# A decode block's result kept as columns, four neighbouring outputs per partition, and stored from there in 8-byte pieces

## The chip, the cores and the metric

One core of a Trainium2 (trn2) chip. The metric is device time in microseconds (us) of one execution. Runs of one kernel mostly agree within 0.3%, with single runs up to 0.5% above that. The profile shows one execution; its span is some 1.8 us shorter than the time of the same run, because the time also counts what lies around the span.

## The reference, cut to what matters

```python
def reference(A_x, A_k_cache, A_v_cache, A_wq, A_wo, B_x, B_w_gate, B_w_up, B_w_down):
    x = A_x                                              # [1, 1, 1024] bf16
    h = x + A_ref(layernorm(x), k_cache, v_cache, wq, wo)  # 32 query heads, 4 kv heads, 65,536 keys of 128
    return h + (gelu(hn @ w_gate) * (hn @ w_up)) @ w_down  # hn = layernorm(h), 3,584 hidden
```

It is one token through one block. Nearly all the work is reading 173 MB: the key and value caches, then the weights. The result is a single vector of 1,024 bf16 values, 2 KB. This document is about how that vector gets formed and stored.

Of the kernel before, what the change touches and what calls it, by code (L numbers as in the profile page):

```python
# [9 lines left out]
ALU = mybir.AluOpType  # L10
AX = mybir.AxisListType
BF16 = mybir.dt.bfloat16
# [5 lines left out]
def kernel(  # L18
# [13 lines left out]
    nc = tc.nc  # L32
    P = 128
    D = A_x.shape[-1]
# [5 lines left out]
    DC = D // P  # L40
# [19 lines left out]
    lead = ctx.enter_context(tc.tile_pool(name="lead", bufs=1))  # L60
    ones_f = lead.tile([P, P], F32, name="ones_f")
    ident_f = lead.tile([P, P], F32, name="ident_f")
    esel = lead.tile([P, 2, P], BF16, name="esel")
    qsel = lead.tile([P, Hkv, 2, 2, 32], BF16, name="qsel")
    hsel = lead.tile([P, 2], F32, name="hsel")
    sel = lead.tile([P, 32], F32, name="sel")
    x_pc = lead.tile([P, DC], F32, name="x_pc")
    x_cp = lead.tile([P, DC], F32, name="x_cp")
    x_row = lead.tile([DC, P], BF16, name="x_row")
    ident_bf = lead.tile([P, P], BF16, name="ident_bf")  # L70
    x_pc_bf = lead.tile([P, DC], BF16, name="x_pc_bf")
    xn_bf = lead.tile([P, DC], BF16, name="xn_bf")
    neg_half = lead.tile([P, 1], F32, name="neg_half")
# [1 line left out]
    xnz = lead.tile([P, DC, 32], BF16, name="xnz")  # L75
    chpool = ctx.enter_context(tc.tile_pool(name="chpool", bufs=NBUF))
    const = ctx.enter_context(tc.tile_pool(name="const", bufs=1))
    small = ctx.enter_context(tc.tile_pool(name="small", bufs=2))
    ps_m = ctx.enter_context(tc.tile_pool(name="ps_m", bufs=1, space=PSUM))
    actx = ExitStack()  # L80
# [9 lines left out]
    def load(src, name):  # L90
        t = chpool.tile([P, CW], BF16, name=name, tag="ch")
        n, w = src.shape[1], src.shape[2]
        tv = t[:, 0:n * w].rearrange("p (n w) -> p n w", w=w)
        nc.sync.dma_start(out=tv, in_=src)
        return tv
# [2 lines left out]
    WB = max(1, CW // HD)  # L98
    assert HD <= CW and DC % WB == 0
    nc.scalar.dma_start(out=x_pc_bf[:], in_=A_x[0, 0].rearrange("(p c) -> p c", c=DC))  # L100
    nc.scalar.dma_start(out=x_row[:], in_=A_x[0, 0].rearrange("(c p) -> c p", p=P))
    wq_tiles = []
    for c0 in range(0, DC, WB):
        wv = load(wq_v[:, c0:c0 + WB, :], "wq_sb")
# [23 lines left out]
    def layernorm_cols(src_col, dst_bf, tagp):  # L128
        s1 = small.tile([P, 1], F32, name=f"{tagp}_s1", tag="ln_s1")
        nc.vector.tensor_reduce(out=s1[:], in_=src_col, axis=AX.X, op=ALU.add)  # L130
        tot = ps_m.tile([P, 1], F32, name=f"{tagp}_tot", tag="misc")
        nc.tensor.matmul(tot[:], lhsT=ones_f[:], rhs=s1[:], start=True, stop=True)
        mean = small.tile([P, 1], F32, name=f"{tagp}_mean", tag="ln_mean")
        nc.vector.tensor_scalar(out=mean[:], in0=tot[:], scalar1=1.0 / D, scalar2=None, op0=ALU.mult)
        xc = small.tile([P, DC], F32, name=f"{tagp}_xc", tag="ln_xc")
        nc.vector.tensor_scalar(out=xc[:], in0=src_col, scalar1=mean[:, 0:1], scalar2=None, op0=ALU.subtract)
        sq = small.tile([P, DC], F32, name=f"{tagp}_sq", tag="ln_sq")
        s2 = small.tile([P, 1], F32, name=f"{tagp}_s2", tag="ln_s2")
        nc.vector.tensor_tensor(out=sq[:], in0=xc[:], in1=xc[:], op=ALU.mult)
        nc.vector.tensor_reduce(out=s2[:], in_=sq[:], axis=AX.X, op=ALU.add)  # L140
        tot2 = ps_m.tile([P, 1], F32, name=f"{tagp}_tot2", tag="misc")
        nc.tensor.matmul(tot2[:], lhsT=ones_f[:], rhs=s2[:], start=True, stop=True)
        ve = small.tile([P, 1], F32, name=f"{tagp}_ve", tag="ln_ve")
        nc.vector.tensor_scalar(out=ve[:], in0=tot2[:], scalar1=1.0 / D, scalar2=eps, op0=ALU.mult, op1=ALU.add)
        rstd = small.tile([P, 1], F32, name=f"{tagp}_rstd", tag="ln_rstd")
        nc.gpsimd.tensor_tensor(out=rstd[:], in0=ve[:], in1=neg_half[:], op=ALU.pow)
        nc.vector.tensor_scalar(out=dst_bf, in0=xc[:], scalar1=rstd[:, 0:1], scalar2=None, op0=ALU.mult)

    nc.vector.tensor_copy(out=x_pc[:], in_=x_pc_bf[:])
    layernorm_cols(x_pc[:], xn_bf[:], "ln1")  # L150
    xT_ps = ps_m.tile([P, DC], BF16, name="xT_ps", tag="misc")
    nc.tensor.transpose(out=xT_ps[:], in_=x_row[:], identity=ident_bf[0:DC, 0:DC])
    nc.vector.tensor_copy(out=x_cp[:], in_=xT_ps[:])

    def padded(pool, vec, ncols, name, t=None):
        if t is None:
# [35 lines left out]
    for hf in range(2):  # L192
        for t in range(2):
            o = W2 * hf + rep * t
            nc.vector.tensor_copy(out=qsel[64 * t:64 * t + 64, :, :, hf, o:o + rep],
                                  in_=qsel_ps[64 * t:64 * t + 64, :, :].rearrange("p a (g h) -> p g a h", h=rep))
# [148 lines left out]
    for dq in range(OQ):  # L345
        nc.tensor.matmul(o2_ps[:], lhsT=osel[:, dq, :], rhs=o_sb[:, dq * Hq:(dq + 1) * Hq],
                         start=(dq == 0), stop=(dq == OQ - 1))

    actx.close()
    rows = ctx.enter_context(tc.tile_pool(name="rows", bufs=1))  # L350
# [7 lines left out]
    def pair_mm(bank, stat, w2, c, first, last):  # L358
        for s in range(DS):
            g = 2 * s + c % 2  # L360
            nc.tensor.matmul(bank[32 * g:32 * g + 32, :], lhsT=stat, rhs=w2[:, s * 512:(s + 1) * 512],  # L361
                             start=first, stop=last, tile_position=(0, 32 * g))
# [6 lines left out]
    for wc in range(Hq // WN):  # L369
        wv = load(wo_v[:, wc * WN:(wc + 1) * WN, :], "wo_sb")  # L370
        for cc in range(WN):
            c = wc * WN + cc
# [4 lines left out]
    for s in range(DS):  # L377
        for c in range(DC):
            nc.tensor.matmul(hc_ps[64 * s:64 * s + 64, c:c + 1], lhsT=at_r[:, c::DC], rhs=hsel[:, s:s + 1],
                             start=True, stop=True, tile_position=(0, 64 * s))  # L380
# [6 lines left out]
    def cp_sum(row, add, name):  # L387
        ps = ps_t.tile([P, 4, DS], F32, name=name + "_ps", tag="T")
        for b in range(4):
            nc.tensor.matmul(ps[:, b, :], lhsT=row[:, b * P:(b + 1) * P], rhs=hsel[:], start=True, stop=True)  # L390
        t = rows.tile([P, DC], F32, name=name)
        nc.vector.tensor_tensor(out=t[:].rearrange("p (s b) -> p b s", b=4), in0=ps[:],
                                in1=add[:].rearrange("p (s b) -> p b s", b=4), op=ALU.add)
        return t

    h_cp = cp_sum(at_r, x_cp, "h_cp")

    assert F <= CW and FC == 28
# [43 lines left out]
    act_bf = rows.tile([P, FC], BF16, name="act_bf")  # L442
# [8 lines left out]
    d_ps = row_bank("d_ps")  # L451
    dl_ps = ps_w.tile([P, DC], F32, name="dl_ps", tag="w")
    nc.vector.memset(dl_ps[:], 0.0)
    o_blk = rows.tile([P, 32], BF16, name="o_blk")
    nc.vector.memset(o_blk[:], 0.0)
    o_tr = rows.tile([32, P], BF16, name="o_tr")
    c0 = 0
    for sz in sizes:
        wv = load(wd_v[:, c0:c0 + sz, :], "wd_sb")
        for cc in range(sz):  # L460
            c = c0 + cc
            if c < NW:
                pair_mm(d_ps, actz[:, c, :], wv[:, cc, :], c, c < 2, c + 2 >= NW)
                continue
            for j in range(DC):
                nc.tensor.matmul(dl_ps[:, j:j + 1], lhsT=wv[:, cc, j * P:(j + 1) * P], rhs=act_bf[:, c:c + 1],
                                 start=False, stop=False, skip_group_check=True)
        c0 += sz
        if c0 == NW:
            d_r = rows.tile([P, 512], F32, name="d_r")  # L470
            nc.vector.tensor_copy(out=d_r[:], in_=d_ps[:])
            hd_cp = cp_sum(d_r, h_cp, "hd_cp")
    nc.vector.tensor_tensor(out=o_blk[:, 0:DC], in0=dl_ps[:], in1=hd_cp[:], op=ALU.add)
    for i in range(4):
        nc.vector.transpose(out=o_tr[:, 32 * i:32 * i + 32], in_=o_blk[32 * i:32 * i + 32, :])
    nc.sync.dma_start(out=out[0, 0].rearrange("(c p) -> c p", p=P), in_=o_tr[0:DC, :])


# [28 lines left out]
```

## The kernel before: the parts that the change touches

The last matrix, `w_down`, comes in five loads of 14, 7, 4, 2 and 1 row groups. The first 14 groups are multiplied with the weights as the moving operand (`d_ps`). The sums of this bank, four partial rows, are turned into columns by `cp_sum` and added to `h`. The last 14 groups arrive too late for that. They use each weight block as the stationary operand and the activation as a single moving column, which gives the result directly as columns: element `c * 128 + p` is in partition `p`, column `c`.

```python
    def cp_sum(row, add, name):
        ps = ps_t.tile([P, 4, DS], F32, name=name + "_ps", tag="T")
        for b in range(4):
            nc.tensor.matmul(ps[:, b, :], lhsT=row[:, b * P:(b + 1) * P], rhs=hsel[:], start=True, stop=True)
        # ... t = ps + add
    # ... (cut)
    for sz in sizes:                                   # 14, 7, 4, 2, 1
        wv = load(wd_v[:, c0:c0 + sz, :], "wd_sb")
        for cc in range(sz):
            c = c0 + cc
            if c < NW:                                 # the first 14
                pair_mm(d_ps, actz[:, c, :], wv[:, cc, :], c, c < 2, c + 2 >= NW)
                continue
            for j in range(DC):                        # DC = 8
                nc.tensor.matmul(dl_ps[:, j:j + 1], lhsT=wv[:, cc, j * P:(j + 1) * P], rhs=act_bf[:, c:c + 1],
                                 start=False, stop=False, skip_group_check=True)
        c0 += sz
        if c0 == NW:
            # ... d_r = copy of d_ps
            hd_cp = cp_sum(d_r, h_cp, "hd_cp")
    nc.vector.tensor_tensor(out=o_blk[:, 0:DC], in0=dl_ps[:], in1=hd_cp[:], op=ALU.add)
    for i in range(4):
        nc.vector.transpose(out=o_tr[:, 32 * i:32 * i + 32], in_=o_blk[32 * i:32 * i + 32, :])
    nc.sync.dma_start(out=out[0, 0].rearrange("(c p) -> c p", p=P), in_=o_tr[0:DC, :])
```

The ending transposes the 128 x 8 result into 8 rows of 128 values with four VectorE instructions, and stores 8 pieces of 256 bytes.

## Time and profile before

| | us |
|---|---|
| median of 3 runs (lowest to highest) | 412.56 (412.27 to 413.38) |
| span of the profiled run | 410.4 |

Some lines of the page of the kernel before come first: busy time by engine with its share of the span, then digits that are tenths in 40 equal slices of the span (the clock granted to TensorE, and the busy share of the DMA engines), then the load queue with packets, MB and share of the span of 16 engines. In these views PE stands for the matmuls of TensorE, PEld for its weight loads, DVE for VectorE, ACT for ScalarE, POOL for GpSimd and SP for SyncE; a `q` after a name is the queue that issues for it, and L361 is line 361 of the kernel.

```profile
PE 296.6 (72%) x2704; PEld 194.9 (47%) x2704; DVE 168.2 (41%) x296; ACT 168.0 (41%) x281; POOL 5.1 (1%) x16
...
PEclk9986999999999999599999966999999585668565
DMA  8999999999999999999999999999999999999994
...
q1 hardware_dynamic: 6496, 173.02, 98.1%
```

The load queue is busy for 98.1% of the span. Until the last weights arrive, the stream sets the pace. Only work after that, or tied with it, can show up in the time.

Next comes the end of the chain of waits of the kernel before: start in us, length in us, what. Pieces of up to 0.04 us between these are left out; what follows in it are the VectorE transposes, which the view below it shows.

```profile
359.31 38.93 DMA wd_sb<-in_B_w_down_dram
...
398.29 3.20 PE d_ps L361 x27
...
401.51 0.70 DVE d_r L471
...
402.26 1.86 PE hd_cp_ps L390 x8
404.12 3.07 PE dl_ps L466 x112
...
407.22 0.18 DVE o_blk L473
```

From the timeline of the same kernel (start, length, engine, line, what, count, idle time before it), the last things that it does:

```profile
403.99 3.20 PE L466 MATMUL dl_ps<-act_bf,wd_sb 128*128 128x1 bf16 x112
...
407.22 0.17 DVE L473 TENSOR_TENSOR o_blk<-dl_ps,hd_cp 128x8 bf16<-128x8 f32 x1 [2.89 <-PE dl_ps L466]
407.42 0.84 DVE L475 STREAM_TRANSPOSE o_tr<-o_blk 32x32 bf16<-32x32 bf16 x4
408.34 0.36 SPq L476 DMA_DIRECT2D out_dram<-o_tr  x1
```

And from the waits of the issuing queue (in all, times, longest, us):

```profile
SPq L502 <- DMA out_dram<-o_tr: 0.5, 1, 0.5
```

What to see: the first `w_down` load lets `d_ps` start at 398.29. From there everything is in series. The add waits for `dl_ps`, the four transposes take 0.84 us, the store is issued at 408.34, and the queue then waits 0.5 us for it before the closing barrier. In the packet records the store's data go out from 409.14 on, and its last semaphore packet ends at 409.22. The queue goes on at 409.56.

### The profile page before, as it was taken

Reading aid. Unit: us, or ns where it says so; the run is one execution under the profiler, and the core shown is the slowest. Engines: PE = TensorE matmul, PEld = TensorE weight load, DVE = VectorE, ACT = ScalarE, POOL = GpSimd, SP = SyncE. Lnnn points to the kernel's source line nnn. Section 1 sums busy time; section 2 is a strip of 40 time slices with the busy share of each in tenths; the row PEclk is TensorE's granted clock in tenths of the full one; section 3 lists DMA queues with packets and bytes.
Section 4 is the critical chain, followed back from the end, with each engine's and each line's share of the span. In section 5 each row is a group of like instructions: output and inputs, shape, how many; then the busy total and the mean of one; then the engine's idle time right before and its main releaser. Section 6 shows DMA issues by size and latency. Waiting matters only on the chain.

```text
span 410.4 us, 6350 instructions
## 1 busy us (share of the span) xinstructions
PE 296.6 (72%) x2704; PEld 194.9 (47%) x2704; DVE 168.2 (41%) x296; ACT 168.0 (41%) x281; POOL 5.1 (1%) x16
## 2 busy tenths in 40 slices
PE   0438989889688987496988929888987466366366
PEld 0216656655366654464566617455654223163134
DVE  0213565557256545255556535456545101021011
ACT  0013766653855654733655634455744700000000
POOL 1100000000000000000000000000000001000000
PEclk9986999999999999599999966999999585668565
DMA  8999999999999999999999999999999999999994
GB/s 358 409 460 407 460 408 457 407 456 412 439 428 423 444 423 442 422 442 410 449 420 444 417 447 420 428 440 414 454 410 453 415 449 418 434 433 436 424 420 172
DMA packets 6684, 173.43 MB, mean 423 GB/s; under 512 B 896, under 2 KB 896, under 8 KB 1152
## 3 DMA queue, kind: packets, MB, share of 16 engines
q1 hardware_dynamic: 6496, 173.02, 98.1%
q8 instruction: 21, 0.34, 0.3%
q14 instruction: 7, 0.06, 0.0%
q10 hardware_dynamic: 160, 0.00, 0.0%
HBM read 173.02 MB, written 0.00 MB: 422 GB/s over the span
## 4 chain that ended last, share of the span: by engine, by line
PE 52%; DMA 24%; DVE 14%; ACT 7%; issue 2%; SPq 0%; DVEq 0%; ACTq 0%
PE kt_ps L223 27%; PE qk_ps L248 11%; DMA wd_sb<-in_B_w_down_dram 9%; DMA k_sb<-in_A_k_cache_dram 7%; DMA wo_sb<-in_A_wo_dram 7%; DVE sc_sb L259 6%; PE acc_ps L303 5%; ACT pT L286 5%; PE sct_ps L256 4%; DVE mx L260 4%; DVE kt_sb L230 3%; ACT qk_sb L253 2%; PE at_ps L361 1%; PE o_ps L319 1%; PE d_ps L361 1%
## 5 line engine op out<-in xcount | busy, mean ns | idle before, releaser
L223 PE MATMUL kt_ps<-ident_f,k_sb 128*128 128x128 f32 x1024 | 148.2, 288 | 17.3 <-DVE kt_sb L230 12.9
L228 ACT COPY kt_sb<-kt_ps 128x1024 bf16<-128x1024 bf16 x116 | 116.4, 1013 | 91.7 <-PE kt_ps L223 63.1
L223 PEld LDWEIGHTS kt_ps<-ident_f,k_sb 128*128 128x128 f32 x1024 | 117.6, 147 | 55.5 <-issue 21.3
L230 DVE COPY kt_sb<-kt_ps 128x1024 bf16<-128x1024 bf16 x140 | 94.7, 687 | 76.1 <-PE qk_ps L248 42.5
L248 PE MATMUL qk_ps<-kt_sb,qsel 128*32 128x512 bf16 x512 | 65.0, 395 | 7.7 <-DVE kt_sb L230 7.7
L259 DVE COPY sc_sb<-sct_ps 128x512 f32<-128x512 f32 x32 | 34.1, 1066 | 46.0 <-PE sct_ps L256 43.7
L286 ACT ACTIVATE pT<-sc_sb,nbias 128x256 bf16<-128x256 f32 x64 | 31.5, 493 | 20.5 <-DVE nbias L278 20.5
L303 PE MATMUL acc_ps<-v_sb,pT 128*32 128x512 bf16 x512 | 33.8, 408 | 3.8 <-DMA v_sb<-in_A_v_cache_dram 3.8
L253 ACT COPY qk_sb<-qk_ps 128x512 f32<-128x512 f32 x32 | 18.8, 589 | 24.9 <-PE qk_ps L248 16.5
L248 PEld LDWEIGHTS <-qsel 128*32 128x32 bf16 x512 | 15.1, 94 | 26.2 <-issue 23.9
L256 PE MATMUL sct_ps<-ident_f,qk_sb 128*128 128x128 f32 x128 | 19.9, 278 | 8.6 <-ACT qk_sb L253 8.6
L303 PEld LDWEIGHTS <-pT 128*32 128x32 bf16 x512 | 14.7, 102 | 18.7 <-issue 7.2
L260 DVE TENSOR_REDUCE mx<-sc_sb 128x8 f32<-128x512 f32 x32 | 22.0, 687 | 1.0
L256 PEld LDWEIGHTS sct_ps<-ident_f,qk_sb 128*128 128x128 f32 x128 | 14.3, 141 | 13.6 <-ACT qk_sb L253 13.6
L172 ACT COPY wg_ev<-wg_ps 96x512 f32<-96x512 f32 x1 | 0.6, 582 | 45.9 <-PE wg_ps L165 45.9
L312 PE MATMUL l_ps<-lpart,ones_f 128*128 128x8 f32 x16 | 3.7, 306 | 15.7 <-ACT pT L286 15.6
L165 PE MATMUL wu_ps<-wu_sb,hnz 128*32 128x512 bf16 x56 | 7.1, 620 | 9.7 <-DMA wu_sb<-in_B_w_up_dram 9.7
L165 PEld LDWEIGHTS <-hnz 128*32 128x32 bf16 x112 | 4.8, 123 | 17.8 <-issue 15.6
L361 PE MATMUL at_ps<-wo_sb,o2z 128*32 128x512 bf16 x64 | 6.6, 590 | 8.6 <-DMA wo_sb<-in_A_wo_dram 8.6
L286 ACT ACTIVATION_READ_ACCUMULATOR pT<-sc_sb,nbias 128x1 f32 x64 | 11.9, 187 | 0.0
L172 ACT ACT_TABLE_LOAD x1 | 1.3, 1283 | 25.0 <-DVE q_ev L170 25.0
L312 PEld LDWEIGHTS l_ps<-lpart,ones_f 128*128 128x128 f32 x16 | 3.0, 234 | 17.8 <-ACT pT L286 17.4
(125 smaller groups left out, 97.7 us busy)
## 6 DMA issues: line engine op xcount, KB each, us to landing
k_sb<-in_A_k_cache_dram SPq DMA_DIRECT2D x16, 4096.0 KB, 27.3
v_sb<-in_A_v_cache_dram SPq DMA_DIRECT2D x16, 4096.0 KB, 21.7
wq_sb<-in_A_wq_dram SPq DMA_DIRECT2D x2, 4096.0 KB, 16.7
wo_sb<-in_A_wo_dram SPq DMA_DIRECT2D x2, 4096.0 KB, 29.7
wg_sb<-in_B_w_gate_dram SPq DMA_DIRECT2D x2, 3584.0 KB, 33.1
wu_sb<-in_B_w_up_dram SPq DMA_DIRECT2D x2, 3584.0 KB, 40.6
wd_sb<-in_B_w_down_dram SPq DMA_DIRECT2D x1, 3584.0 KB
wd_sb<-in_B_w_down_dram SPq DMA_DIRECT2D x1, 1792.0 KB, 29.6
```

The source lines that it names most:

```text
L165: nc.tensor.matmul(banks[s // 4][32 * g:32 * g + 32, :], lhsT=stat, rhs=mov(s), start=first, stop=last, tile_position=(0, 32 * g))
L223: nc.tensor.transpose(out=kt_ps[:, b, :], in_=k32s[m0 // 16][:, m0 % 16, :], identity=ident_f[:])
L228: nc.scalar.copy(out=dst_bf, in_=src_bf)
L230: nc.vector.tensor_copy(out=dst_bf, in_=src_bf)
L248: nc.tensor.matmul(qk_ps[32 * c:32 * c + 32, :], lhsT=qsel[:, g, par, hf, :], rhs=mv[:, :, :, par], start=(hf == 0 and par == 0), stop=(hf ...
L253: nc.scalar.copy(out=qk_sb[:], in_=qk_ps[:])
L256: nc.tensor.transpose(out=sct_ps[:, b, :], in_=qk_sb[:, b * P:(b + 1) * P], identity=ident_f[:])
L259: nc.vector.tensor_copy(out=sl.rearrange("p h (m t) -> p m t h", t=2), in_=src_v)
L260: nc.vector.tensor_reduce(out=st["mx"][:, :, pi], in_=sl, axis=AX.X, op=ALU.max)
L286: nc.scalar.activation(out=pT[:, :, r, :], in_=sc_sb[:, r, hf * HG * TG:(hf + 1) * HG * TG].rearrange("p (a t) -> p a t", t=TG), func=ACT. ...
L303: nc.tensor.matmul(acc[32 * c:32 * c + rep * TG, :], lhsT=pTs[a // HG][:, a % HG, :, :].rearrange("p r t -> p (r t)"), rhs=v_sb[:, i * TG: ...
L361: nc.tensor.matmul(bank[32 * g:32 * g + 32, :], lhsT=stat, rhs=w2[:, s * 512:(s + 1) * 512], start=first, stop=last, tile_position=(0, 32 ...
```

## The change

The intent is to drop the transposes by making the columns storable. If partition `p` holds outputs `4p` to `4p + 3` of each half of the vector, its eight values are two runs of 8 bytes in memory, and a store can take them from where they are. For that, the weights must be read with a column step of 4: in `dl_ps`, in `cp_sum`, and in the layout of `x`. Two small tiles move to another pool to make room.

```diff
-    x_row = lead.tile([DC, P], BF16, name="x_row")
+    x_row = lead.tile([2, D // 2], BF16, name="x_row")
 ... (esel and ident_bf move from pool lead to pool const)
-    nc.tensor.transpose(out=xT_ps[:], in_=x_row[:], identity=ident_bf[0:DC, 0:DC])
+    for e in range(4):
+        nc.tensor.transpose(out=xT_ps[:, e, :], in_=x_row[:, e::4], identity=ident_bf[0:2, 0:2])
 ... (cut: the load of x_row, the shape of xT_ps and its copy)
-            nc.tensor.matmul(ps[:, b, :], lhsT=row[:, b * P:(b + 1) * P], rhs=hsel[:], start=True, stop=True)
+            nc.tensor.matmul(ps[:, b, :], lhsT=row[:, b::4], rhs=hsel[:], start=True, stop=True)
 ...
-                nc.tensor.matmul(dl_ps[:, j:j + 1], lhsT=wv[:, cc, j * P:(j + 1) * P], rhs=act_bf[:, c:c + 1],
+                nc.tensor.matmul(dl_ps[:, j:j + 1], lhsT=wv[:, cc, (j // 4) * 512 + j % 4:(j // 4 + 1) * 512:4], rhs=act_bf[:, c:c + 1],
 ...
-    nc.vector.tensor_tensor(out=o_blk[:, 0:DC], in0=dl_ps[:], in1=hd_cp[:], op=ALU.add)
-    for i in range(4):
-        nc.vector.transpose(out=o_tr[:, 32 * i:32 * i + 32], in_=o_blk[32 * i:32 * i + 32, :])
-    nc.sync.dma_start(out=out[0, 0].rearrange("(c p) -> c p", p=P), in_=o_tr[0:DC, :])
+    nc.vector.tensor_tensor(out=o_col[:], in0=dl_ps[:], in1=hd_cp[:], op=ALU.add)
+    nc.sync.dma_start(out=out[0, 0].rearrange("(s p e) -> p s e", p=P, e=4),
+                      in_=o_col[:].rearrange("p (s e) -> p s e", e=4))
```

More of the change, by code (lines that the diff above doesn't have):

```diff
@@ L62 @@
     ident_f = lead.tile([P, P], F32, name="ident_f")
-    esel = lead.tile([P, 2, P], BF16, name="esel")
     qsel = lead.tile([P, Hkv, 2, 2, 32], BF16, name="qsel")
@@ L68 @@
     x_cp = lead.tile([P, DC], F32, name="x_cp")
-    x_row = lead.tile([DC, P], BF16, name="x_row")
-    ident_bf = lead.tile([P, P], BF16, name="ident_bf")
+    x_row = lead.tile([2, D // 2], BF16, name="x_row")
     x_pc_bf = lead.tile([P, DC], BF16, name="x_pc_bf")
@@ L77 @@
     const = ctx.enter_context(tc.tile_pool(name="const", bufs=1))
+    esel = const.tile([P, 2, P], BF16, name="esel")
+    ident_bf = const.tile([P, P], BF16, name="ident_bf")
     small = ctx.enter_context(tc.tile_pool(name="small", bufs=2))
@@ L100 @@
     nc.scalar.dma_start(out=x_pc_bf[:], in_=A_x[0, 0].rearrange("(p c) -> p c", c=DC))
-    nc.scalar.dma_start(out=x_row[:], in_=A_x[0, 0].rearrange("(c p) -> c p", p=P))
+    nc.scalar.dma_start(out=x_row[:], in_=A_x[0, 0].rearrange("(s n) -> s n", s=2))
     wq_tiles = []
@@ L150 @@
     layernorm_cols(x_pc[:], xn_bf[:], "ln1")
-    xT_ps = ps_m.tile([P, DC], BF16, name="xT_ps", tag="misc")
-    nc.tensor.transpose(out=xT_ps[:], in_=x_row[:], identity=ident_bf[0:DC, 0:DC])
-    nc.vector.tensor_copy(out=x_cp[:], in_=xT_ps[:])
+    xT_ps = ps_m.tile([P, 4, 2], BF16, name="xT_ps", tag="misc")
+    for e in range(4):
+        nc.tensor.transpose(out=xT_ps[:, e, :], in_=x_row[:, e::4], identity=ident_bf[0:2, 0:2])
+    nc.vector.tensor_copy(out=x_cp[:].rearrange("p (s e) -> p e s", e=4), in_=xT_ps[:])
     def padded(pool, vec, ncols, name, t=None):
@@ L453 @@
     nc.vector.memset(dl_ps[:], 0.0)
-    o_blk = rows.tile([P, 32], BF16, name="o_blk")
-    nc.vector.memset(o_blk[:], 0.0)
-    o_tr = rows.tile([32, P], BF16, name="o_tr")
+    o_col = rows.tile([P, DC], BF16, name="o_col")
     c0 = 0
```

## The prediction

> **What bounds the kernel now.** The page: DMA queue at 98% of the span, 423 GB/s; up to the last weight loads the stream decides. The chain of waits shows what follows. The first down-projection load lands at 398.25 us; then, in series: d_ps matmuls 3.20 us, d_r eviction 0.70, eight hd_cp matmuls 1.86, 112 dl_ps matmuls 3.07 (start to start 26.7 ns, granted clock 0.50), o_blk add 0.17, four DVE transposes 0.84, store issue 0.36 at 408.34, its packets at 409.14 to 409.21, end 410.4. The DMA packets show the last load ending at 406.43; TensorE stops only some 50 ns for it at 406.8. So TensorE and the stream are tied there, and what follows 407.2 is pure tail.
>
> **What the change does.**
> 1. Removes the four transposes: 407.42 to 408.26, **-0.85 us**, all on the critical path.
> 2. The store becomes 128 partitions x 2 pieces of 8 bytes instead of 8 rows of 256. The 16-byte packets of the x load took about 9 ns each; 256 pieces over 16 engines: 16 x 9 = 0.15 us (estimate) against 0.07 now. The Trainium skill, "DMA: Bandwidth & Descriptors" (Specifications), has writes under 512 B as read-modify-write; the present rows are under it already, at 15 to 20 ns. **+0.1 to +0.4 us**, on the path.
> 3. The 112 weight loads of dl_ps read columns 8 bytes apart instead of 2. This is the real risk, wholly on the path. For: the skill, "TensorE: Matmul & The Clock Gate" (Weight-path perf modes), lets fast weight load take "packed or strided" columns; 26.7 ns for 128 says that it is on now. Gate matmuls at full clock read 8-byte runs 56 bytes apart, four side by side every 220 ns or so. Against: float32 loads here do pay for strides: transposes of 128 columns go every 122 ns with a 16-byte step (wg_t) against 109 packed (qt_ps, both clock 1.0), and 64 columns with a 32-byte step (hc_ps) take 120. If that is 17 bytes of span per ns and fast loads share it, 1,024 bytes cost 60 ns and dl_ps gains 112 x 33 = 3.7 us (estimate). No slowdown: two chances in three.
> 4. hd_cp and h_cp read float32 rows 16 bytes apart: at clock 0.50 the packed form already takes 213 ns a load, above 122. No change.
> 5. Start: four small transposes of x_row instead of one, under the wait for xnz (TensorE idle 1.28 us). Buffers move between pools without changing which loads wait. Nothing.
>
> **Sum.** Without stride cost: about -0.65 us, 411.9; with it about +3, 415.6. My point is **412.1 us**, range **411.2 to 415.6**. Faster by over 2%: 0.01; within 2%: 0.96; slower by over 2%: 0.03.
>
> **What would show each step.** Tail: store issue about 0.1 us after the add. Store: 256 packets of 8 bytes, about 9 ns each, last by 0.9 us after issue. dl_ps: 26.7 ns start to start if right, 60 if the rival holds. hd_cp: still 213 ns. First 398 us unchanged; d_ps starts within 0.5 us of 398.3.
>
> **What would make it wrong.** Strided bf16 weight loads slower than packed (fast load lost, 107 ns each: +9 us, just over 2%); 8-byte writes much dearer than 9 ns or completing late; the last load landing later, because stragglers decide the tie at 406.8; a shifted SBUF layout altering the stream (three runs spread 1.1 us).

## The result, and the profile after

| | before | changed |
|---|---|---|
| median of 4 runs, us | 412.50 | 414.16 |
| lowest to highest, us | 412.27 to 413.38 | 413.92 to 414.31 |
| ratio, 95% interval | | 1.0036 (1.0018 to 1.0053) |
| span of the profiled run, us | 410.4 | 412.4 |

A ratio is the mean time of one kernel's fast runs over that of the other's of the same rounds, so it is not quite the ratio of the medians. The difference is far inside 2%, but it is clear of noise, and it is a loss.

The chain of waits of the changed kernel, its end:

```profile
359.76 38.69 DMA wd_sb<-in_B_w_down_dram
...
398.49 3.20 PE d_ps L362 x22
...
401.71 0.70 DVE d_r L470
...
402.46 2.03 PE hd_cp_ps L391 x8
404.49 3.74 PE dl_ps L465 x112
...
408.25 0.17 DVE o_col L472
```

The timeline of the changed kernel, the same last things:

```profile
404.35 3.86 PE L465 MATMUL dl_ps<-act_bf,wd_sb 128*128 128x1 bf16 x112
...
408.25 0.17 DVE L472 TENSOR_TENSOR o_col<-dl_ps,hd_cp 128x8 bf16<-128x8 f32 x1 [3.55 <-PE dl_ps L465]
408.49 0.40 SPq L473 DMA_DIRECT2D out_dram<-o_col  x1
```

And its queue's wait for the store:

```profile
SPq L500 <- DMA out_dram<-o_col: 2.4, 1, 2.4
```

The transposes are gone, and the store is issued 0.24 us after the add started, against 1.12. But `dl_ps` takes longer, and the queue waits 2.4 us for a store of the same 2 KB. The store's completion is the interval from the end of its last packet until the queue goes on. The two tails side by side, from the starts in the two timelines and from the packet records:

| step | before | changed | difference |
|---|---|---|---|
| start of `d_ps` (the stream decides) | 398.29 | 398.49 | +0.20 |
| `d_ps` start to `hd_cp` start | 3.97 | 3.97 | 0.00 |
| `hd_cp` start to first `dl_ps` matmul | 1.73 | 1.89 | +0.16 |
| `dl_ps` to the add | 3.23 | 3.90 | +0.67 |
| add to issue of the store | 1.12 | 0.24 | -0.88 |
| issue to end of the last packet | 0.88 | 1.17 | +0.29 |
| the store's completion | 0.35 | 1.95 | +1.60 |
| from there to the end of the span | 0.81 | 0.81 | 0.00 |
| **sum** | | | **+2.04** |

The sum is the difference of the spans, 2.0 us. The saving came as planned and was paid back three times over: 0.83 us by strided weight loads, 1.89 us by the store. The +0.20 of the first row is where the stream stood in these two traces; the medians differ by 1.66 us.

The trace also records each landing that a store reports to its semaphore, and these show how the completion grew. The kernel before has 8 landings, between 0.26 and 0.33 us after the last packet. The changed kernel has 16: the first comes after 0.31 us too, but the others follow one after another, in groups, until 1.93 us.

### The profile page after: what moved, and what is told of

The parts are those of the page before. It is cut to its first block, busy times and chain, and to the rows that moved or that the text cites. A ratio compares the mean times of both kernels' runs of the same rounds, so it can differ in the third digit from the quotient of the medians.

```text
span 412.4 us, 6350 instructions
## 1 busy us (share of the span) xinstructions
PE 301.0 (73%) x2707; PEld 196.7 (48%) x2707; DVE 167.7 (41%) x291; ACT 168.1 (41%) x281; POOL 5.2 (1%) x16
## 4 chain that ended last, share of the span: by engine, by line
PE 52%; DMA 23%; DVE 14%; ACT 7%; issue 2%; SPq 0%; ACTq 0%; DVEq 0%
PE kt_ps L224 27%; PE qk_ps L249 11%; DMA wd_sb<-in_B_w_down_dram 9%; DMA k_sb<-in_A_k_cache_dram 7%; DMA wo_sb<-in_A_wo_dram 6%; DVE sc_sb L260 6%; PE acc_ps L304 5%; ACT pT L287 5%; PE sct_ps L257 4%; DVE mx L261 4%; DVE kt_sb L231 3%; ACT qk_sb L254 2%; PE dl_ps L465 1%; PE at_ps L362 1%; PE o_ps L320 1%
## 5 line engine op out<-in xcount | busy, mean ns | idle before, releaser
L249 PEld LDWEIGHTS <-qsel 128*32 128x32 bf16 x512 | 15.1, 94 | 26.7 <-issue 24.4
L173 ACT ACT_TABLE_LOAD x1 | 1.3, 1283 | 26.7 <-DVE q_ev L171 26.7
```

The lines of the kernel that those rows point to most:

```text
L249: nc.tensor.matmul(qk_ps[32 * c:32 * c + 32, :], lhsT=qsel[:, g, par, hf, :], rhs=mv[:, :, :, par], start=(hf == 0 and par == 0), stop=(hf ...
```

## The experiments

**Which half costs what.** My theory was that both halves of the change cost time, independently. Each half was then run alone. Both kernels permute the output on purpose and are therefore wrong.

*e1_strided_loads_row_store*: the changed kernel with the old ending.

```diff
-    nc.vector.tensor_tensor(out=o_col[:], in0=dl_ps[:], in1=hd_cp[:], op=ALU.add)
-    nc.sync.dma_start(out=out[0, 0].rearrange("(s p e) -> p s e", p=P, e=4), ...)
+    nc.vector.tensor_tensor(out=o_blk[:, 0:DC], in0=dl_ps[:], in1=hd_cp[:], op=ALU.add)
+    # ... four transposes into o_tr, and
+    nc.sync.dma_start(out=out[0, 0].rearrange("(c p) -> c p", p=P), in_=o_tr[0:DC, :])
```

> The changed kernel with the old ending put back: four DVE transposes and a store of 8 rows of 256 bytes (output permuted on purpose, so wrong). Theory (both halves of the change cost): only the strided weight loads remain, so dl_ps stays at 33.3 ns start to start and hd_cp at 233 ns, together +0.67 +0.17, and the store completes about 0.36 us after its last packet, as before: 0.84 us over the kernel before, about 413.3 us. Rival (the store alone made the loss, the 33.3 ns were an accident of that trace): dl_ps back at 26.7, the time of the kernel before, 412.5 us.

*e2_packed_loads_8byte_store*: the kernel before with the changed ending only.

```diff
-    nc.vector.tensor_tensor(out=o_blk[:, 0:DC], in0=dl_ps[:], in1=hd_cp[:], op=ALU.add)
-    # ... four transposes, store of 8 rows
+    nc.vector.tensor_tensor(out=o_col[:], in0=dl_ps[:], in1=hd_cp[:], op=ALU.add)
+    nc.sync.dma_start(out=out[0, 0].rearrange("(s p e) -> p s e", p=P, e=4), ...)
```

> The kernel before with only its ending changed: no transposes, store of 256 pieces of 8 bytes (output permuted on purpose, so wrong). Theory: dl_ps at 26.7 ns, -0.88 us of transposes, and the store's +0.29 us to its last packet and +1.60 us from there to the wait's end: +1.0 us, about 413.5 us. Rival (late completion came from something else in the changed kernel, such as the moved buffers): wait ends 0.36 us after the last packet, total about 0.6 us under the kernel before, 411.9 us.

| | before, same rounds | e1 | e2 |
|---|---|---|---|
| median, us | 412.38 | 413.25 | 413.50 |
| ratio, 95% interval | | 1.0024 (1.0011 to 1.0037) | 1.0035 (1.0019 to 1.005) |
| `hd_cp`, ns start to start | 213 | 233 | 213 |
| `dl_ps`, ns start to start | 26.7 | 33.3 | 26.7 |
| the store's completion, us | 0.35 | 0.35 | 2.08 |

(The three lower values of the kernel before are from its first profile.) The timeline of e1:

```profile
404.41 3.87 PE L467 MATMUL dl_ps<-act_bf,wd_sb 128*128 128x1 bf16 x112
...
408.51 0.84 DVE L476 STREAM_TRANSPOSE o_tr<-o_blk 32x32 bf16<-32x32 bf16 x4
```

And its queue's wait for the store:

```profile
SPq L503 <- DMA out_dram<-o_tr: 0.5, 1, 0.5
```

The timeline of e2 follows. Its profiled run was its longest, with `d_ps` starting 2 us late in the stream, so only lengths are read from it:

```profile
406.20 3.21 PE L464 MATMUL dl_ps<-act_bf,wd_sb 128*128 128x1 bf16 x112
...
409.69 0.41 SPq L472 DMA_DIRECT2D out_dram<-o_col  x1
```

And its queue's wait for the store:

```profile
SPq L499 <- DMA out_dram<-o_col: 2.5, 1, 2.5
```

The slow `dl_ps` goes with the strided loads, and the long wait goes with the 8-byte store. The losses, 0.87 and 1.12 us, add up to 1.99, against 1.6 to 1.7 us for the whole change in its own rounds. With the scatter of single runs that is as near as these data get. Both rivals fail.

**Why the store completes late.**

*e3_store_sweep*: the kernel before, and after its own store a series of stores to a scratch tensor, each of which waits for the one before it (correct output).

```diff
+    scr = nc.dram_tensor("probe_scratch", (N_S,), BF16, kind="Internal").ap()
+    for rnd in range(2):
+        probe_spe()                 # 256 x 8 B, as the changed kernel stores
+        probe(8, 1, 128)            # 8 x 256 B, as the kernel before stores
+        probe(1, 1, 4)              # one piece of 8 B
+        # ... and so on, each an nc.sync.dma_start
```

> The kernel before, followed by 13 stores to a scratch tensor, each waiting for the one before, twice over. 256 pieces of 8 bytes as in the change should show about 2.0 us from the last packet to the wait's end, 8 rows of 256 bytes about 0.36. Three readings of why. Same memory line (neighbouring pieces queue for one line): 256 pieces 512 bytes apart end within about 0.5 us, and 16-, 32- and 64-byte pieces step down as fewer share a line. Any short write is late: one single 8-byte piece also takes about 2.0. Number of short pieces: 256 apart also take 2.0, 128 about half of it, 16 almost nothing.

From the packet records and the issue times: us from the end of a store's last packet to the issue of the next, first and second time. (The very first store ran beside the kernel's own, here and in the next sweep.)

| pieces | us | pieces | us |
|---|---|---|---|
| 256 x 8 B, the change's order | 2.05, 2.89 | 128 x 16 B | 0.39, 1.77 |
| 8 x 256 B | 0.35, 0.35 | 64 x 32 B | 0.36, 0.37 |
| 1 x 8 B | 0.33, 0.32 | 32 x 64 B | 0.35, 0.36 |
| 16 x 8 B, adjacent | 0.35, 0.34 | 16 x 128 B | 0.35, 0.35 |
| 128 x 8 B, adjacent | 2.74, 3.89 | 128 x 64 B | 0.38, 0.38 |
| 256 x 8 B, 512 B apart | 0.43, 0.44 | 128 x 512 B | 0.36, last |

(Another store, 4 x 512 B, took 0.35 both times.) A single short write is not late. As many short writes as in the change are not late either when they lie apart. Only neighbouring ones are, and these were late in a scratch tensor too, so the output tensor is not the cause. That leaves the first of the three readings, with a share of the third: 16 neighbours were on time, 128 were not. Its forecast for piece sizes did not come out as a series of steps: 32-byte pieces are already on time, and 16-byte pieces were late in one of two.

*e7_gap_sweep*: 128 pieces of 8 bytes at growing distances, four times over (correct output).

```diff
+    for rnd in range(4):
+        for gap in (4, 8, 16, 32, 64, 128, 256, 512):      # elements of 2 bytes
+            probe(gap)
```

> The kernel before, then stores of 128 pieces of 8 bytes whose starts are 8, 16, 32, 64, 128, 256, 512 and 1,024 bytes apart, four times over, each waiting for the one before. If pieces queue for a shared memory line, the wait after the last packet is 2 to 4 us at 8 bytes and falls to 0.35 us once the distance reaches the line: at 32 or 64 bytes. If it is a matter of a memory page or a channel, only at 512 bytes or more. If the wait depends on the number of short pieces, it is the same at every distance.

The same interval, in us, four times:

| distance | 8 B | 16 B | 32 B | 64 B | 128 B to 1,024 B |
|---|---|---|---|---|---|
| us | 2.01, 1.75, 1.75, 1.69 | 0.39, 0.94, 1.00, 0.78 | 0.39, 1.04, 0.71, 0.39 | 0.40, 0.39, 0.40, 0.40 | 0.38 to 0.39 |

The lateness ends at 64 bytes, where no two pieces share a 64-byte stretch any more. This held in all four rounds. The distance is what was measured; that the stretch is one of 64 bytes is read from it.

*e8_changed_pieces_64_apart* and *e9_changed_again*: the same test in the changed kernel itself, beside the unaltered changed kernel in the same rounds. In e8 the output gets only a copy of `x`.

```diff
+    nc.scalar.dma_start(out=out[0, 0].rearrange("(s n) -> s n", s=2), in_=x_row[:])   # at the start
 ...
-    nc.sync.dma_start(out=out[0, 0].rearrange("(s p e) -> p s e", p=P, e=4),
+    nc.sync.dma_start(out=scr.rearrange("(s p e) -> p s e", p=P, e=32)[:, :, 0:4],
                       in_=o_col[:].rearrange("p (s e) -> p s e", e=4))
```

> The changed kernel with one thing different: the same 256 pieces of 8 bytes go, from the same tile and in the same order, to a scratch tensor with 64 bytes from one piece to the next (the output only gets a copy of x at the start, so it is wrong on purpose). If pieces wait for each other where they share 64 bytes of memory, the wait after the last packet falls from 1.95 to about 0.4 us and the kernel is about 1.6 us under the changed kernel, near 412.6 us. If many short pieces are late wherever they go, it stays at 414.2.

> The changed kernel as it is, on the same chip and in the same rounds as the one above: 414.2 us, 1.004 of the kernel before; hd_cp at 233 ns and dl_ps at 33.3 ns start to start again, and the wait after the store's last packet again 1.5 to 2.5 us.

| | before | e8 | e9 |
|---|---|---|---|
| median, us | 412.30 | 412.68 | 413.93 |
| ratio, 95% interval | | 1.0004 (0.9991 to 1.0016) | 1.0035 (1.0021 to 1.0049) |
| the store's completion, us | | 0.49 | 1.74 |

The wait of e8's queue for its store:

```profile
SPq L502 <- DMA probe_scratch<-o_col: 1.0, 1, 1.0
```

The same 256 pieces from the same tile, 64 bytes apart instead of adjacent, take 1.25 us off both the completion and the kernel. That is somewhat less than the 1.6 expected, because the completion was shorter in e9 than in the first profile. In e8 all 16 landings come between 0.25 and 0.43 us after the last packet; in e9 the last one comes after 1.72. `hd_cp` took 233 ns and `dl_ps` 33.3 in both. With the lateness gone, the changed kernel ties with the kernel before: what the transposes had cost is then spent on the strided loads.

**What a column step costs a weight load.**

*e4_load_sweep*: the kernel before, then groups of weight loads, each load followed by a matmul of one column (bf16) or two (float32), on constant data (correct output).

```diff
+        probe_bf("b_step1", wsrc[:, 0:128], 64)
+        probe_bf("b_step4", wsrc[:, 0:512:4], 64)
+        # ... steps 2, 8, 16
+        probe_f32("f_step4", fsrc[:, 0:512:4], 8)
+        # ... steps 1, 2, 8, and 64 columns at steps 1 and 8
```

> The kernel before, followed by groups of weight loads at steps of 1, 2, 4, 8, 16 columns in bfloat16 and 1, 2, 4, 8 in float32, each with a matmul of one or two columns, three times over so that both clocks appear. Theory (the read is limited by the span that it covers): bfloat16 step 1 and 2 at the array's pace (26.7 ns at clock 0.5), step 4 at 33 ns at any clock, step 8 about 65, step 16 about 130; float32 step 4 at 233 ns at any clock, step 8 about twice that. Rival (a strided load costs a fixed extra, whatever its step): steps 2, 4, 8 and 16 all about 33 ns.

The table gives matmul starts, one to the next, in ns, at granted clock 0.50, from the second and third time (in the first, the scheduler mixed the probes with the kernel's own matmuls). A float32 matmul shows as two passes here, and the number is for one pass.

| 128 columns, step | 1 | 2 | 4 | 8 | 16 |
|---|---|---|---|---|---|
| bf16, bytes from column to column | 2 | 4 | 8 | 16 | 32 |
| bf16, ns | 26.7 | 26.7 | 33.3 | 60.0 | 61.7 |
| float32, bytes from column to column | 4 | 8 | 16 | 32 | |
| float32, ns | 213 | 213 | 233 | 238 | |

From the busy times by window in this run (length, then PE and PEld busy time with counts, other engines, granted clock, DMA), the windows lie within bf16 steps 2, 4, 8 and 16:

```profile
439.30:440.90 1.60, 1.60 (x67) 1.60 (x64) 0.95 (x5) 0.00 (x0) 0.00 (x0) 0.50 0.00 0
441.00:443.00 2.00, 2.00 (x66) 2.00 (x64) 0.00 (x0) 0.00 (x0) 0.00 (x0) 0.50 0.05 9
443.20:446.80 3.60, 3.60 (x64) 3.60 (x63) 0.00 (x0) 0.00 (x0) 0.00 (x0) 0.50 0.00 0
447.00:450.80 3.80, 3.80 (x65) 3.80 (x65) 0.00 (x0) 0.00 (x0) 0.00 (x0) 0.50 0.02 4
```

About the same number of matmuls takes 1.6, 2.0, 3.6 and 3.8 us. The 33.3 ns of the changed kernel is thus the plain cost of a step of 4. The cost does not follow the span as my theory said (step 16 would have been 130 ns), nor is it a fixed extra as the rival said. It grows until every column lies in its own 16 bytes and then stays. The numbers fit a cost for each 16-byte line touched: 64 lines in 33.3 ns, 128 lines in 60.0. That fit is not proved by anything else, and it is one for bf16 alone: 128 lines in float32 take 233 to 238 ns. At clock 1.00 a step of 1 took 25 ns (the kernel's own `dl_ps` in e3) and a step of 4 took 33 (the first matmuls of `dl_ps` in the changed kernel). Loads of 64 float32 columns took 107 ns at step 1 and 120 at step 8.

The float32 loads do not depend on the clock when strided: `hd_cp` went at 233 ns in the profile of the changed kernel, at clock 1.00, and also in e9, at 0.50. Packed they do: 213 ns at 0.50 in the kernel before, and 112 ns in this run, where the kernel's own `hd_cp` fell in a stretch at 1.00.

**A version meant to beat both.** From the sweep, pieces of 64 bytes complete on time. One transpose of the whole 128 x 32 block leaves 32 pieces of 64 bytes, with packed loads. Both forms are correct.

*e6_one_transpose_64byte_store*:

```diff
-    nc.vector.tensor_tensor(out=o_blk[:, 0:DC], in0=dl_ps[:], in1=hd_cp[:], op=ALU.add)
-    for i in range(4):
-        nc.vector.transpose(out=o_tr[:, 32 * i:32 * i + 32], in_=o_blk[32 * i:32 * i + 32, :])
-    nc.sync.dma_start(out=out[0, 0].rearrange("(c p) -> c p", p=P), in_=o_tr[0:DC, :])
+    nc.vector.tensor_tensor(out=o_blk[:, 0:32:4], in0=dl_ps[:], in1=hd_cp[:], op=ALU.add)
+    nc.vector.transpose(out=o_tr[:], in_=o_blk[:])                     # o_tr is [128, 32] here
+    nc.sync.dma_start(out=out[0, 0].rearrange("(c i l) -> i c l", i=4, l=32), in_=o_tr[0:128:4, :])
```

> The kernel before with packed loads, one DVE transpose of 128x32 instead of four of 32x32, and one store of 32 pieces of 64 bytes; correct output. From the sweep: three transposes of 0.21 us gone (-0.63), the store's last packet about 0.1 us later, its wait ends about 0.35 us after that: about 0.5 us under the kernel before, 411.9 us, and 2.2 us under the changed kernel. If late completion sets in for pieces of 64 bytes next to each other too (rival: any short neighbouring piece), 1 us or more over the kernel before.

*e5_one_transpose_four_stores*:

```diff
+    nc.vector.transpose(out=o_tr[:], in_=o_blk[:])
+    for i in range(4):
+        eng = nc.sync if i % 2 == 0 else nc.scalar
+        eng.dma_start(out=out_v[i], in_=o_tr[32 * i:32 * i + DC, :])
```

> The same single transpose, stored by four DMAs of 8 pieces of 64 bytes from two issuing queues; correct output. -0.63 us, but the second issue on each queue comes about 0.4 us after the first: about 0.2 us under the kernel before, 412.2 us; with a late completion as above 1 us or more over it.

Medians: 412.33 us for e6 and 412.46 for e5, against 412.54 for the kernel before, both ratios 1.0 (e6 0.9983 to 1.0016, e5 0.9985 to 1.0016). Neither gain showed. The timeline of e6 says where its gain went:

```profile
407.28 0.18 DVE L473 TENSOR_TENSOR o_blk<-dl_ps,hd_cp 128x8 bf16<-128x8 f32 x1 [2.97 <-PE dl_ps L466]
407.49 0.21 DVE L474 STREAM_TRANSPOSE o_tr<-o_blk 128x32 bf16<-128x32 bf16 x1
407.78 0.69 SPq L475 DMA_DIRECT2D out_dram<-o_tr  x1
```

One transpose takes 0.21 us instead of 0.84, as wanted, and the completion is 0.36 us. But the issue of this store takes 0.69 us instead of 0.36, and its first packet comes 1.29 us after it instead of 0.80. With the pattern of 4 x 8 runs in memory against 32 partitions, the first packet is 0.49 us later, and that eats most of the 0.63. The size and number of the pieces alone are not the cause: in e3, 32 pieces of 64 bytes in a plain pattern were issued in 0.33 us, with the first packet after 0.82. What in the pattern costs the time was not tested. In e5 the second store of the SyncE queue was issued 0.42 us after the first, as expected, and from the add to the end of the span it took 3.34 us against 3.15 before. Some 0.3 us of that are the queue's own: it looks at the store's semaphore first, and only then at five others, some 0.06 us each, which it goes through while the store is under way in the kernel before.

## Why the prediction was right or wrong, point by point

- **Size.** The range held (414.16 in 411.2 to 415.6), and it is the same within 2%, as forecast. The point, 412.1, was 2.1 us too low and had the wrong sign: it foretold a gain of 0.4 us where 1.66 us were lost. That the range held was luck. Its upper end stood there for `dl_ps` at 60 ns, +3.7 us, which did not come; the largest loss was the completion, for which the sum had no term. And "within 2%", 8.2 us, was easily right for a change in the last 12 us.
- **Step 1, the transposes ("-0.85 us, all on the critical path").** Right: -0.88 from add to issue.
- **Step 2, the store ("+0.1 to +0.4 us").** This is the term that failed most: +1.89. The part that I costed was right within its range: +0.29 to the last packet, of which the 256 packets of 8 bytes at 7 to 9 ns each account for +0.17 (0.25 us from the first to the last, against 0.08) and a later first packet for the rest. I left the completion at its old length, and it grew by 1.60 (1.74 to 2.08 us in all in other runs, against 0.35). The prediction named it only under what would make it wrong ("completing late"). e2, e7 and e8 show what took its place: many 8-byte pieces less than 64 bytes apart complete late.
- **Step 3, strided bf16 loads ("No slowdown: two chances in three").** Wrong, though the rival put beside it was wrong too: 33.3 ns, not 26.7 and not 60; +0.67 us on the path, not 3.7. The 60 ns belong to a step of 8.
- **Step 4, `hd_cp` ("above 122. No change").** Wrong by +0.16: it takes 233 ns. The 122 ns came from float32 transposes, and the float32 matmuls did not go at that pace; why was not tested. At clock 0.50 the packed 213 hides nearly all of the difference. At clock 1.00, where packed takes 112, it would not, but there the stream set the end instead. The trace of e3 shows it, where the kernel before ran `hd_cp` at 1.00: `dl_ps` began 0.85 us sooner after the start of `d_ps` than in the first profile, then waited for its weights (the bracket at the end of a line gives the idle time and what ended it), and the add came 8.98 us after the start of `d_ps`, against 8.94.

```profile
403.42 1.54 PE L466 MATMUL dl_ps<-act_bf,wd_sb 128*128 128x1 bf16 x56
...
405.24 1.01 PE L466 MATMUL dl_ps<-act_bf,wd_sb 128*128 128x1 bf16 x32 [0.28 <-DMA wd_sb<-in_B_w_down_dram]
...
406.50 1.01 PE L466 MATMUL dl_ps<-act_bf,wd_sb 128*128 128x1 bf16 x24 [0.24 <-DMA wd_sb<-in_B_w_down_dram]
```

- **Step 5, start and pools.** Held: `d_ps` started at 398.49 against 398.29, and 398.43 in e9.
- **The tie at 406.8.** Still there without strided loads: in the trace of e6 `dl_ps` pauses at 406.7 for the last load. With strided loads TensorE runs past it.

What stays open: how the memory handles neighbours. 16 adjacent pieces of 8 bytes were on time, so a distance under 64 bytes is needed for the lateness but is not enough. Those 16 pieces had 16 semaphore packets, one for each piece, where the late stores have one for 8 or 16 pieces; whether that or the plain number of neighbours decides was not tested. The length also varies from run to run, and from one pass of a sweep to the next, for 16 and 32 bytes of distance.

## What to carry to other kernels

A store that ends a kernel is paid until its completion, so read the wait after its last packet and not only its packets: here 2 KB in 8-byte neighbours cost more than the transposes that made rows of them. When a layout is changed to save work at the end, list every read that must now be strided, and measure a step on the same kind of instruction before taking its cost from another. A saving of a few tenths of a microsecond is easily eaten by a more complicated DMA pattern: 0.49 of 0.63 us in e6.

## What the Trainium skill lacked or had wrong

- "SBUF — State Buffer", section "Door 1: The DMA port swizzle (why `[64,N]` ≈ `[32,N]`)", says of 16-byte lines that one can stride for free up to 4 float32 or 8 bf16. For weight loads this differs: a bf16 step of 4 costs 33.3 ns against 26.7, a step of 8 costs 60.0, and a float32 step of 4 costs 233 against 213 at clock 0.50 (233 against 112 at 1.00). Its picture of 16-byte lines does fit the levelling off at steps of 8 and 16 (60.0 and 61.7).
- "TensorE: Matmul & The Clock Gate", section "Weight-path perf modes — Fast Weight Load (FWL) and DoubleRow", allows "packed or strided" columns for fast weight load, and gives no cost of the stride. It is the same 33.3 and 60.0 ns.
- "DMA: Bandwidth & Descriptors", section "Specifications", warns of read-modify-write below 512 B in general. Here 64-byte and 256-byte pieces, and lone 8-byte pieces 64 bytes or more apart, completed 0.32 to 0.44 us after their last packet in the sweeps. Only many pieces of 8 bytes less than 64 bytes apart, and in one of two passes neighbouring pieces of 16 bytes, were late, by up to 3.9 us after the last packet.
- The same page, section "Anatomy of one DMA — SWDGE (gpsimd) path", puts most of a fixed 2 us on the write receipt, for DMAs issued from GpSimd. These stores, issued from SyncE, took 0.88 us to the last packet and 0.35 us from there. No section gives a figure for what a more complicated pattern costs the issue on this path: 0.69 us against 0.36 in e6, and the first packet 0.49 us later.
